# Attention, weight decoding and a first feed-forward pass: an order of issue computed in the kernel, in place of fixed offsets

## The chip, the cores and the metric

The kernel runs on one core of one Trainium2 chip. The metric is the time of one execution on the device in microseconds (us), the median of three runs. The engines are PE (TensorE; PEld are its weight loads), DVE (VectorE), ACT (ScalarE), POOL (GpSimd) and SP (SyncE, which here issues the DMAs).

## The reference

The result of a linear attention goes through a feed-forward layer with squared ReLU, and that through a mixture of eight experts whose gates come from a Sinkhorn iteration. All inputs are float32; only the weights of the first layer come as float64, which the kernel sees as pairs of 32-bit integers and turns into float32 itself ("decoding").

```python
# q, k, v: (4, 8, 576, 64), w_phi: (64, 128)
def phi(x):
    proj = x @ w_phi
    proj = proj - max(abs(proj), axis=-1)
    return concatenate([exp(proj), exp(-proj)], -1)
kv = einsum('bhsf,bhsd->bhfd', phi(k), v);  z = sum(phi(k), axis=2)
attn = einsum('bhsf,bhfd->bhsd', phi(q), kv) / (phi(q) @ z + 1e-6)
x = attn as (2304, 512)
x = relu(x @ w_in) ** 2 @ w_out              # w_in (512, 2048), w_out (2048, 512)
P = exp(x @ w_gate - max); 8 times: divide by row sums, by column sums, times N / E
out = sum over e of P[:, e] * (relu(x @ w1[e]) @ w2[e])   # 8 experts, 1024 hidden
```

## The kernel before

**Attention.** There are 16 units: four batches times four pairs of heads. A unit turns its keys (`turn_k`: PE transposes into pskT; high and low parts kh and kl), projects them (`proj_k`: PSUM tiles psk of two token tiles each; DVE takes the largest absolute value mk and subtracts it; ACT makes both exponentials in ek), sums them over the tokens (`kv_sum`: kvp with v, zp with ones) and turns the sums (`kv_turn`: kzp; kv, zs, z). Its queries are split (`split_q`: qst), turned (`turn_q`: psqT, qT), projected in four half-length pieces (`proj_q`: psq; POOL's all-reduce over partitions finds the maximum, DVE subtracts, ACT makes the exponentials eq). `numerators` makes, for each half of the tokens, psn and then psd; `recip` gathers the denominators from dn to comp by DMA, inverts them, writes them to DRAM (rden) and reads them back spread over the partitions (rb); `finish` multiplies (nm) and writes the high and low parts xh (ACT) and xl (DVE) of the next layer's input. Products in float32 precision are made of two or three products of high and low parts (`mm3`, lines 244 to 246).

**Decoding.** `decode` turns one 128-row block of a float64 weight into float32 with seven DVE instructions (lines 198 to 204); there are eight blocks for each of the four feed-forward passes. `split_w` makes high and low parts.

**The passes.** Each pass takes 512 of the 2048 hidden features. The first one works on eight halves of 288 tokens: `first_l1` makes four hidden tiles (48 matmuls), `first_l2` four output tiles (48), stored to `part` in DRAM. The passes behind it work on 512 tokens at a time, and the experts follow at line 874.

**The order.** An attention unit's ten steps are listed with offsets (`OFFS`), each unit `TU` = 17.54 us after the one before; the steps of all units are sorted by that time and emitted. Decoding follows the units named in `DECU`, right behind their `finish`. First-pass halves are emitted after them; `HOLD` ties some of them behind the key sums of a later unit. The framework then orders each engine's queue by its own estimate of times. PSUM for attention is two pools of three banks, shared in turn by all its tiles, and two banks for the first pass.

Of the kernel before, what the change touches and what calls it, by code (L numbers as in the profile page):

```python
# [10 lines left out]
I32 = mybir.dt.int32  # L11
# [9 lines left out]
def tile_features_attention__moe__sinkhorn_moe(  # L21
# [36 lines left out]
    GT = 2  # L58
    EQB = 4
    PAB, PCB = 3, 3  # L60
    NMB = 1
    EKB = 3
    STB = 1
    QTB = 1
    KTB = 1
    VAB = 2
    NQB = 1

    EARLY = {(0, 'kp'): -1, (0, 'qst'): -1}

    QSA = (0, 1)

    PIPE = (3, 4, 5,)
    TU = 17.54

    DECU = [1, 2, 3, 3, 4, 6, 7, 7, 9, 9, 9, 12, 12, 14, 14, 14]
    HOLD = {1: (4, "kvi"), 2: (12, "kvi"), 3: (15, "kvi"), 4: (12, "kvi"), 5: (10, "kvi")}
    OFFS = [(0, 'kT'), (3.4, 'kp'), (1.59, 'qst'), (3.0, 'qT'), (6.83, 'qp'), (9.28, 'kv'), (13.57, 'kz'), (23.24, 'num'), (31.33, 'rec'), (39.32, 'fin')]
# [12 lines left out]
    hp = hp1.enter_context(tc.tile_pool(name="hp1", bufs=1, side="right", reuse_waits="tile"))  # L91
    a1 = ctx.enter_context(ExitStack())
    ab = a1.enter_context(tc.tile_pool(name="ab", bufs=1, reuse_waits="tile"))
    pa = a1.enter_context(tc.tile_pool(name="pa", bufs=PAB, space=PSUM, reuse_waits="tile"))
    pc = a1.enter_context(tc.tile_pool(name="pc", bufs=PCB, space=PSUM, reuse_waits="tile"))
# [12 lines left out]
    nat = {}  # L108
# [7 lines left out]
    def load_q(u):  # L116
        if u >= NU:
            return
        t = ab.tile([P, NT2, D], F32, tag="nq", bufs=NQB, name="qnat")
        nc.sync.dma_start(t, heads(q, u).rearrange("h s d -> (h s) d").rearrange("(t p) d -> p t d", p=P))  # L120
        nat["q", u] = t

    def load_kv(u, src, nm, bufs):

        if u >= NU:
            return
        t = ab.tile([P, MT + 1, 2, D], F32, tag=f"n{nm}", bufs=bufs, name=f"{nm}nat")
        src = heads(src, u)
        for h in range(2):
            nc.sync.dma_start(t[:, :MT, h], src[h, : MT * P].rearrange("(p t) d -> p t d", t=MT))  # L130
        nc.sync.dma_start(t[:R0, MT], src[:, MT * P :].rearrange("h p d -> p h d"))
        nat[nm, u] = t

    def load_k(u):
        load_kv(u, k, "k", 2)

    def load_v(u):
        load_kv(u, v, "v", VAB)

    load_k(0)  # L140

    stg = ab.tile([P, 3, NF], F32, tag="ek", bufs=EKB, name="stg")
# [3 lines left out]
    load_q(0)  # L146
    load_v(0)
    load_k(1)
# [33 lines left out]
    def load_raw(p, w, i):  # L182
        t = wr.tile([P, FB, 2], I32, tag="raw", bufs=2, name=f"raw{p}_{w}_{i}")
        nc.sync.dma_start(t.rearrange("p f w -> p (f w)"), passes[p][w][i * P : (i + 1) * P, :])
        raws[p, w, i] = t

    def decode(p, w, i):


        raw = raws.pop((p, w, i))  # L190
        lo, hi = raw[:, :, 0], raw[:, :, 1]
        if i == 0:
            wf[p, w] = stage(p, w)
        sf = wf[p, w][:, i]
        s = sf.bitcast(I32)
        m = wr.tile([P, FB], I32, tag="dm", name="dm")
        mf = m.bitcast(F32)
        nc.vector.tensor_scalar(m, hi, 3, 0x3FFFFFF8, ALU.logical_shift_left, ALU.bitwise_and)
        nc.vector.scalar_tensor_tensor(m, hi, -0x40000000, m, ALU.bitwise_and, ALU.bitwise_or)
        nc.vector.tensor_scalar(s, m, -0x800000, None, ALU.bitwise_and)  # L200
        nc.vector.scalar_tensor_tensor(sf, lo.bitcast(U32), 2.0**-52, sf, ALU.mult, ALU.mult)
        nc.vector.tensor_add(sf, mf, sf)
        nc.vector.tensor_scalar(m, hi, 0x7FFFFFFF, None, ALU.bitwise_and)
        nc.vector.scalar_tensor_tensor(sf, m, float(897 << 20), sf, ALU.is_ge, ALU.mult)

    def fetch(p):

        if p >= NP:
            return
        if p >= N1:  # L210
            for w in range(2):
                wf[p, w] = stage(p, w)
                nc.sync.dma_start(wf[p, w], passes[p][w].rearrange("(k p) f -> p k f", p=P))
                yield
            return
        order = [(w, i) for w in range(2) for i in range(KD)]
        load_raw(p, *order[0])
# [8 lines left out]
    def split_w(p, w):  # L226
# [15 lines left out]

    def mm3(ps, ah, al, bh, bl, first, last):
        nc.tensor.matmul(ps, ah, bh, start=first, stop=False)  # L244
        nc.tensor.matmul(ps, ah, bl, start=False, stop=False)  # L245
        latest["pe"] = nc.tensor.matmul(ps, al, bh, start=False, stop=last).ins  # L246
# [13 lines left out]
    HB = {"hh": 5, "hl": 5, "r": 1}  # L260

    def split_square(pool, ps, n, nmax):

        r = pool.tile([P, nmax], F32, tag="r", bufs=HB["r"], name="r")
        nc.scalar.activation(r[:, :n], ps[:, :n], AF.Relu)  # L265
        nc.vector.tensor_mul(r[:, :n], r[:, :n], r[:, :n])
        gh = pool.tile([P, nmax], F32R, tag="hh", bufs=HB["hh"], name="gh")
        gl = pool.tile([P, nmax], F32R, tag="hl", bufs=HB["hl"], name="gl")
        latest["act"] = nc.scalar.copy(gh[:, :n], r[:, :n]).ins
        latest["dve"] = nc.vector.tensor_sub(gl[:, :n], r[:, :n], gh[:, :n].bitcast(F32)).ins  # L270
# [12 lines left out]
    def split_q(u):  # L283

        t = nat.pop(("q", u))
        st = ab.tile([P, NT2, 2, D], F32R, tag="st", bufs=STB, name="qst")
        (nc.scalar.copy if u in QSA else nc.gpsimd.tensor_copy)(st[:, :, 0], t)
        nc.vector.tensor_sub(st[:, :, 1], t, st[:, :, 0].bitcast(F32))
        load_q(u + NQB)
        return st  # L290

    def turn_q(st):
        tr = ab.tile([P, NT2, P], F32R, tag="qT", bufs=QTB, name="qT")
        for g in range(0, NT2, 4):
            n = min(4, NT2 - g)
            ps = pa.tile([P, 4, P], F32R, tag="pa", name="psqT")
            for i in range(n):
                nc.tensor.transpose(ps[:, i], st[:, g + i].rearrange("p a d -> p (a d)"), ident_r)
            nc.scalar.copy(tr[:, g : g + n], ps[:, :n].bitcast(F32))
        return tr  # L300

    def turn_k(u):
        t = nat.pop(("k", u))
        kh = ab.tile([P, S], F32R, tag="kT", bufs=KTB, name="kh")
        kl = ab.tile([P, S], F32R, tag="kl", bufs=KTB, name="kl")
        for i0, n in ((0, MT), (MT, 1)):
            ps = pa.tile([P, MT * P], F32, tag="pa", name="pskT")
            w = n * P if n > 1 else R0
            for i in range(n):
                r = P if n > 1 else R0  # L310
                nc.tensor.transpose(ps[:, i * P : i * P + r], t[:r, i0 + i].rearrange("p h d -> p (h d)"), ident[:r, :r])
            cs = slice(i0 * P, i0 * P + w)
            nc.scalar.copy(kh[:, cs], ps[:, :w])
            nc.vector.tensor_sub(kl[:, cs], ps[:, :w], kh[:, cs].bitcast(F32))
        load_k(u + 2)
        return kh, kl

    def proj_k(kT):

        eks = []  # L320
        for g in range(0, MT + 1, GT):
            n, r = (GT, P) if g < MT else (1, R0)
            ek = ab.tile([P, GT, 2, 2, NF], F32, tag="ek", bufs=EKB, name="ek")
            pk, nk = ek[:r, :n, :, 0], ek[:r, :n, :, 1]
            ps = pa.tile([P, GT, 2, NF], F32, tag="pa", name="psk")
            for i in range(n):
                cs = slice((g + i) * P, (g + i) * P + r)
                mm3(ps[:r, i], kT[0][:, cs], kT[1][:, cs], wdh, wdl, True, True)
            mk = ab.tile([P, GT, 2, 1], F32, tag="mk", bufs=2, name="mk")
            nc.vector.tensor_reduce(mk[:r, :n], ps[:r, :n], AX.X, ALU.max, apply_absolute_value=True)  # L330
            nc.vector.tensor_sub(pk, ps[:r, :n], mk[:r, :n].to_broadcast([r, n, 2, NF]))
            nc.scalar.activation(nk, pk, AF.Exp, scale=-1.0)
            nc.scalar.activation(pk, pk, AF.Exp)
            eks.append(ek)
        return eks

    def kv_sum(u, eks):


        t = nat.pop(("v", u))  # L340
        kvp = pc.tile([P, 512], F32, tag="pc", name="kvp")
        zp = pc.tile([P, 512], F32, tag="pc", name="zp")

        def rows(i, h):
            r = P if i < MT else R0
            return r, eks[i // GT][:r, i % GT, h].rearrange("p a f -> p (a f)")

        for g in range(0, MT + 1, 2):
            tiles = range(g, min(g + 2, MT + 1))
            for i in tiles:  # L350
                for h in range(2):
                    r, e = rows(i, h)
# [780 lines left out]
```

## Time and profile before

| | |
|---|---|
| runs | 2089.14, 2089.8, 2092.29 us; median 2089.8 |
| span of the profiled execution | 2090.2 us |
| its own time | not listed apart from the runs |
| PE busy, weight loads busy | 99%, 92% of the span |
| DVE, ACT, POOL busy | 83%, 42%, 37% |
| instructions | 31752 |

The span runs from the first to the last instruction of the profiled execution. Matmuls are pipelined and their ends are modelled, so PE's busy time contains waiting; the weight loads show better how densely it works. A row of a timeline gives start, length, engine, line, operation and the tiles (out<-in); a duration there reaches to the modelled end.

### The profile page before, as it was taken

What the parts mean: (1) busy time and instruction counts of PE and PEld (TensorE: products, weight loads), DVE (VectorE), ACT (ScalarE), POOL (GpSimd) and SP (SyncE); (2) the same over time, 40 slices, a digit from 0 to 9 for tenths busy, and PEclk for the clock granted to TensorE, in tenths of its full rate; (3) what the DMA queues carried; (4) which work ended last, traced back from release to release, by engine and by line L of the source; (5) the groups of instructions that cost most, each with busy time, mean ns of one, the idle gap of its engine ahead of it and who ended that gap; (6) DMA issues with size and microseconds to landing.
All of it is one profiled execution on the core that took longest, in us unless ns stands there. A gap on an engine that the chain in (4) does not pass through costs nothing.

```text
span 2090.2 us, 31752 instructions
## 1 busy us (share of the span) xinstructions
PE 2060.6 (99%) x12411; PEld 1924.6 (92%) x12411; DVE 1736.2 (83%) x2138; ACT 872.6 (42%) x1503; POOL 771.7 (37%) x428
## 2 busy tenths in 40 slices
PE   8999999999999999999999999999999999999998
PEld 5556679888999999999999999999999999999998
DVE  4888665766557898999989999899998989989986
ACT  6786754222233654343333434334333433433332
POOL 3343300010104544354534545345453444534431
PEclk9999999999999999999999999999999999999999
DMA  4444222110135566676666676676766776767663
GB/s 113 112 106 119 75 81 88 57 31 31 56 138 206 207 238 201 227 238 229 217 230 241 223 223 223 226 244 219 227 226 220 242 215 231 226 224 245 205 203 122
DMA packets 182949, 375.23 MB, mean 180 GB/s; under 512 B 73360, under 2 KB 113168, under 8 KB 182800
## 3 DMA queue, kind: packets, MB, share of 16 engines
q1 hardware_dynamic: 182800, 373.20, 54.4%
q8 instruction: 99, 1.62, 0.3%
q14 instruction: 50, 0.41, 0.1%
HBM read 348.67 MB, written 24.34 MB: 178 GB/s over the span
## 4 chain that ended last, share of the span: by engine, by line
PE 87%; DVE 7%; DMA 3%; ACT 1%; issue 1%; SPq 0%; POOL 0%; DVEq 0%; ACTq 0%
PE psa L874 31%; PE psb L874 31%; PE ps L244 6%; PE ps L245 6%; PE ps L246 6%; PE kvp L353 1%; DMA rb<-rden 1%; PE psn L409 1%; DVE acc L990 1%; DVE xl L610 1%; PE zp L360 1%; DMA rden<-comp 1%; DVE w2v L610 1%; PE psd L418 1%; PE psg L651 1%
## 5 line engine op out<-in xcount | busy, mean ns | idle before, releaser
L874 PE MATMUL psa<-xl,xh 128*128 128x384 f32 x2400 | 446.0, 335 | 3.5 <-DVE xl L610 2.5
L874 PE MATMUL psb<-xl,xh 128*128 128x384 f32 x2400 | 445.9, 335 | 3.5 <-DVE mu L949 1.8
L874 PEld LDWEIGHTS psb<-xl,xh 128*128 128x128 f32 x2400 | 419.1, 188 | 4.5 <-DVE mu L949 2.1
L874 PEld LDWEIGHTS psa<-xl,xh 128*128 128x128 f32 x2400 | 418.6, 188 | 4.7 <-DVE xl L610 2.9
L902 POOL TENSOR_TENSOR t<-r,r 128x768 f32<-128x768 f32 x96 | 207.2, 2158 | 500.5 <-DVE r L942 453.8
L902 POOL TENSOR_TENSOR t<-r,t 128x768 f32<-128x768 f32 x96 | 236.1, 2460 | 7.4 <-ACT r L946 1.9
L610 DVE TENSOR_TENSOR xl<-t,xl 128x768 fp32r<-128x768 f32 x128 | 186.9, 1460 | 1.8 <-ACT xl L609 1.6
L990 DVE TENSOR_TENSOR acc<-psb,acc 128x768 f32<-128x768 f32 x163 | 155.0, 951 | 35.6 <-PE psb L874 32.1
L990 DVE TENSOR_TENSOR acc<-psa,acc 128x768 f32<-128x768 f32 x161 | 153.1, 951 | 37.1 <-PE psa L874 33.9
L874 PE MATMUL psb<-xl,w2v 128*128 128x384 f32 x960 | 180.2, 334 | 0.0
L874 PE MATMUL psa<-xl,w2v 128*128 128x384 f32 x960 | 180.1, 334 | 0.0
L609 ACT CAST xl<-t 128x768 fp32r<-128x768 f32 x128 | 107.2, 838 | 156.6 <-POOL t L902 66.5
L874 PEld LDWEIGHTS psa<-xl,w2v 128*128 128x128 f32 x960 | 167.5, 188 | 0.0
L874 PEld LDWEIGHTS psb<-xl,w2v 128*128 128x128 f32 x960 | 167.5, 188 | 0.0
L609 ACT CAST xl<-r 128x768 fp32r<-128x768 f32 x96 | 80.4, 838 | 155.7 <-PE psa L874 77.4
L393 POOL PARTITION_ALL_REDUCE eq<-eq x64 | 90.7, 1460 | 138.4 <-ACT eq L392 138.4
L610 DVE TENSOR_TENSOR xl<-r,xl 128x768 fp32r<-128x768 f32 x96 | 135.9, 1416 | 1.4 <-ACT xl L609 1.4
L244 PE MATMUL ps<-xh,w0h 128*128 128x288 f32 (+3 forms) x384 | 130.5, 341 | 0.9 <-ACT r L265 0.8
L245 PE MATMUL ps<-xl,w0h 128*128 128x288 f32 (+3 forms) x384 | 129.0, 336 | 0.0
L246 PE MATMUL ps<-xh,w0l 128*128 128x288 f32 (+3 forms) x384 | 128.3, 337 | 0.0
L245 PE MATMUL ps<-gl,w1h 128*128 128x288 f32 (+3 forms) x384 | 126.9, 338 | 0.0
L246 PE MATMUL ps<-gh,w1l 128*128 128x288 f32 (+3 forms) x384 | 126.5, 338 | 0.0
(196 smaller groups left out, 3736.7 us busy)
## 6 DMA issues: line engine op xcount, KB each, us to landing
xl<-xv SPq DMA_DIRECT2D x329, 768.0 KB
wf<-in_moe_w_dram SPq DMA_DIRECT2D x32, 1024.0 KB
gate<-prT SPq DMA_DIRECT2D x45, 384.0 KB
xv<-xvs SPq DMA_DIRECT2D x14, 768.0 KB
raw<-in_moe_w_in_dram SPq DMA_DIRECT2D x16, 512.0 KB
raw<-in_moe_w_out_dram SPq DMA_DIRECT2D x16, 512.0 KB
xv<-xl SPq DMA_DIRECT2D x7, 768.0 KB
qnat<-in_q_dram SPq DMA_DIRECT2D x16, 288.0 KB
```

The source lines that it names most:

```text
L244: nc.tensor.matmul(ps, ah, bh, start=first, stop=False)
L245: nc.tensor.matmul(ps, ah, bl, start=False, stop=False)
L246: latest["pe"] = nc.tensor.matmul(ps, al, bh, start=False, stop=last).ins
L353: nc.tensor.matmul(kvp[h * D : (h + 1) * D, : 2 * NF], t[:r, i, h], e, start=(i == 0), stop=(i == MT))
L360: ins = nc.tensor.matmul(zp[q0 : q0 + 32, : 2 * NF], ones[:r, :32], e, start=(i < 2), stop=(i >= MT - 1))
L393: nc.gpsimd.partition_all_reduce(eq[:, 1], eq[:, 0], P, bass_isa.ReduceOp.absmax)
L409: nc.tensor.matmul(ps[h * D : (h + 1) * D, :HALF], kv[:, a, h * D : (h + 1) * D], eqs[2 * c + h][:, a], start=(a == 0), stop=(a == 1),)
L609: nc.scalar.copy(v[:, 0], src)
L610: nc.vector.tensor_sub(v[:, 1], src, v[:, 0].bitcast(F32))
L874: ins = nc.tensor.matmul(ps[:, x, :NB], w[:, wi, k, cs], b[:, bi, k], start=first and k + i == 0, stop=k == KH - 1 and i == 2, skip_group_ ...
L902: nc.gpsimd.tensor_tensor(t[nm], x, y, ALU.subtract)
L990: latest["dve"] = nc.vector.tensor_add(o, ps, o).ins
```

## The change

The steps of attention, the decoding of the first two passes' weights, and the first pass's work on six of the eight halves (five of them whole, of the sixth the hidden tiles) become steps of a list. Each has an engine, an assumed duration, what it needs, which PSUM slot it takes and a key. A scheduler in the kernel's Python simulates the engines: at each turn it takes the engine that can start first and gives it the ready step with the smallest key. The steps are emitted in that order, and each instruction of PE, DVE, ACT, POOL and SP is tied behind the one before it on its engine.

PSUM for attention becomes named tiles: two of two banks ("w") and two of one bank ("s"), each chosen by the scheduler; two banks ("m") stay for the first pass and the turned key sums.

The steps themselves change too:
- Keys: the rest of 64 tokens of both heads is loaded as one 128-row tile (with each head twice, side by side), so that five whole transposes do, and its projection takes two matmuls with `wks`. The load takes six DMAs where there were three; v's rest goes to zero-padded tiles, four DMAs where there were three. Maximum, subtraction and exponentials run on five and on four column blocks of 128 rather than on three pieces.
- Queries: projection, copy, all-reduce, subtraction and exponentials run once per head on 576 columns rather than on four pieces of 288. POOL makes the high part of q for all units.
- Numerators and denominators run once over both halves; denominators add up in PSUM, so one DMA gathers them. The copy of kv moves from DVE to ACT, those of z and of xh to POOL.
- Decoding gets another sequence of seven instructions; for the first pass it runs on two blocks at once. For the third and fourth passes' weights (decoded during the second and third), two of the seven steps go to POOL.
- One all-reduce on POOL runs at the start.

The core of the diff (removed functions are printed above):

```diff
+    class InOrder:
+        def __getattr__(self, name):
+            made = getattr(self.engine, name)
+            def op(*args, **how):
+                with ExitStack() as es:
+                    if ordered[0] and self.key in queued:
+                        es.enter_context(tc.issue_after(queued[self.key]))
+                    ins = made(*args, **how)
+                queued[self.key] = ins.ins
+                return ins
+            return op
+    V = InOrder(nc.vector, "dve")
+    A = InOrder(nc.scalar, "act")
+    G = InOrder(nc.gpsimd, "pool")
...
+    def decode_ops(lo, hi, sf, m, E):
+        s, mf = sf.bitcast(I32), m.bitcast(F32)
+        return [
+            lambda: V.tensor_scalar(m, hi, 0x7FFFFFFF, None, ALU.bitwise_and),
+            lambda: E.tensor_scalar(mf, mf, 2.0**-15, None, ALU.max),
+            lambda: V.tensor_scalar(m, m, 3, 0x3FFFFFF8, ALU.logical_shift_left, ALU.bitwise_and),
+            lambda: V.scalar_tensor_tensor(m, hi, -0x40000000, m, ALU.bitwise_and, ALU.bitwise_or),
+            lambda: V.tensor_scalar(s, m, -0x800000, None, ALU.bitwise_and),
+            lambda: V.scalar_tensor_tensor(sf, lo.bitcast(U32), 2.0**-52, sf, ALU.mult, ALU.mult),
+            lambda: E.tensor_add(sf, mf, sf),
+        ]
...
+    LAT = {"PE": 0.30, "DVE": 0.07, "ACT": 0.07, "POOL": 0.10, "SP": 0.07}
+    RINGS = {"w": 2, "s": 2, "m": 2}
+    EARLY, LATE = 15.02, 15.53
...
+    START = {"PE": 9.0, "DVE": 7.5, "ACT": 7.5, "POOL": 6.0, "SP": 3.5}
...
+        while len(made) < len(steps):
+            best = None
+            for e, todo in known.items():
+                at = [(room(s), s) for s in todo]
+                at = [(r, s) for r, s in at if r is not None]
+                if not at:
+                    continue
+                t = max(free[e], min(r for r, _ in at))
+                now = min(((s.key, s.index, max(r, t), s) for r, s in at if r <= t))
...
+                if best is None or now[2] < best[0]:
+                    best = now[2:]
+            t, s = best
...
+            free[e] = t + s.dur
+            s.end = t + s.dur + LAT[e]
+            if s.kb:
+                dma = max(dma, t + 1.7) + s.kb / 190.0
+                s.end = dma + 0.4
...
+        base = EARLY * min(u, 5) + LATE * max(0, u - 5)
+        def step(nm, *args, **how):
+            add(n(nm), *args, key=base + PHASE[nm], **how)
...
+        step("ldk", "SP", 0.36, loads_k, [n("tk", u - 1)], kb=295)
+        step("ldq", "SP", 0.06, loads_q, [n("qhi", u - 1), n("qlo", u - 1)], kb=295)
+        step("ldv", "SP", 0.24, loads_v, [n("A", u - 1)], kb=295)
...
+        step("A", "PE", 3.25, sums, [n("epA"), n("epB"), n("ldv")], [], ("s",), ([n("kvs")],), cols=1)
...
+        step("psn", "PE", 2.04, numerators, [n("qp0_"), n("qp1_"), n("kvc")], [], ("w",), ([n("nm")],), cols=1
+        )
+        step("psd", "PE", 1.2, denominators, [n("qp0_"), n("qp1_"), n("zw")], [n("psn")], ("s",), ([n("dn")],), cols=1)
+        step("cmp", "SP", 0.06, to_comp, [n("dn"), n("rd", u - 1)], kb=20)
+        step("rec", "DVE", 0.38, recip, [n("cmp")])
+        step("rd", "SP", 0.06, to_dram, [n("rec")], kb=20)
+        step("rb", "SP", 0.12, to_rows, [n("rd"), n("mul", u - 1)], kb=150)
+        step("mul", "DVE", 0.76, mul, [n("rb"), n("nm")])
+        step("xhi", "POOL", 0.75, xhi, [n("mul")] + raws_of)
+        step("xlo", "DVE", 0.75, xlo, [n("xhi")] + raws_of)
...
+                f"L1_{m}", "PE", 1.6, l1, xs_ + ["sl0", "sl2"], l2_of + ([f"L1_{m - 1}"] if m else []),
+                ("m",), ([f"re{m}"],), key=1e4 + 10 * seq,
...
+    plan = schedule()
+    for s in plan:
+        now[0] = s
+        s.emit()
+    ordered[0] = False
```

## Rows read from the trace of the kernel before

**Rows 1.** The page's slices (40 equal parts of the span), busy tenths of weight loads.

```profile
PEld 5556679888999999999999999999999999999998
```

**Rows 2.** Stretches: start:end, length, busy us and instructions of each engine, clock, DMA.

```profile
20.00:80.00 60.00, 58.17 (x465) 33.97 (x466) 40.78 (x92) 48.77 (x129) 28.83 (x23) 1.00 0.40 90
80.00:290.00 210.00, 202.30 (x1594) 132.10 (x1590) 167.09 (x345) 148.31 (x383) 71.87 (x57) 0.98 0.37 97
...
366.00:440.00 74.00, 74.00 (x373) 63.25 (x372) 46.78 (x83) 16.36 (x30) 0.00 (x0) 1.00 0.12 39
```

**Rows 3.** Timeline of PE, 0 to 60 us: start, length, what.

```profile
4.79 1.38 PE L311 MATMUL pskT<-ident,knat 128*128 128x128 f32 x5 [4.79 <-DMA knat<-in_k_dram]
...
20.53 0.80 PE L311 MATMUL pskT<-ident,knat 128*128 128x128 f32 x5
...
46.15 0.60 PE L311 MATMUL pskT<-ident,knat 128*128 128x128 f32 x4
46.68 2.53 PE L353 MATMUL kvp<-ek,vnat 128*64 128x256 f32 x20
49.14 0.27 PE L311 MATMUL pskT<-ident,knat 64*128 64x64 f32 x1
...
49.81 1.62 PE L360 MATMUL zp<-ek,ones 128*32 128x256 f32 x20
51.36 0.54 PE L298 MATMUL psqT<-ident_r,qst 128*128 128x128 f32 x4
...
52.33 0.28 PE L246 MATMUL psk<-wdh,kl 128*128 128x256 f32 x1
52.45 0.28 PE L244 MATMUL psk<-wdh,kh 128*128 128x256 f32 x1
...
54.15 1.19 PE L409 MATMUL psn<-eq,kv 128*64 128x288 f32 x8
55.27 0.40 PE L389 MATMUL psq<-qT,wks 128*128 128x288 f32 x1
55.51 0.29 PE L390 MATMUL psq<-qT,wks 128*128 128x288 f32 x1
...
59.14 0.69 PE L418 MATMUL psd<-eq,z 128*32 128x288 f32 x8
59.76 0.40 PE L389 MATMUL psq<-qT,wks 128*128 128x288 f32 x1
```

**Rows 4.** Timeline of PE: first and last of 48 first-pass matmuls back to back.

```profile
299.93 0.30 PE L244 MATMUL ps<-xh,w0h 128*128 128x288 f32 x1
...
306.14 0.29 PE L246 MATMUL ps<-xh,w0l 128*128 128x288 f32 x1
```

**Rows 5.** A stretch, instructions with tile ps (the first pass) alone: PE, PEld, DVE, ACT.

```profile
0.00:290.00 290.00, 57.41 (x336) 47.28 (x336) 0.00 (x0) 11.08 (x27) 0.99 0.39 100
```

**Rows 6.** DVE groups to 345 us: busy, mean ns, idle before; last: min/median/max.

```profile
L394 DVE TENSOR_TENSOR eq<-eq 128x288 f32<-128x288 f32 x64 | 33.7, 529 | 7.2 <-POOL eq L393 7.2
...
L439 DVE TENSOR_TENSOR nm<-nm,rb 128x576 f32<-128x576 f32 x16 | 12.6, 786 | 17.1 <-DMA rb<-rden 17.1
...
L442 DVE TENSOR_TENSOR xl<-nm,xh x16: 736/758/1282, 48.1 to 322.1; 128x576 fp32r<-128x576 f32 x16
```

**Rows 7.** Timeline of SP's issues at the start.

```profile
0.72 1.34 SPq L130 DMA_DIRECT2D knat<-in_k_dram  x2
2.10 0.63 SPq L131 DMA_DIRECT2D knat<-in_k_dram  x1
```

**Rows 8.** The page's costliest groups: POOL's two-input sums in the expert stage.

```profile
L902 POOL TENSOR_TENSOR t<-r,t 128x768 f32<-128x768 f32 x96 | 236.1, 2460 | 7.4 <-ACT r L946 1.9
```

**Rows 9.** The chain that ended last, 60 to 78 us: the transfers of one unit's denominators.

```profile
62.20 2.15 DMA comp<-dn
...
66.67 2.12 DMA rden<-comp
...
69.36 4.48 DMA rb<-rden
```

More of the change, by code (lines that the diff above doesn't have):

```diff
@@ L114, in heads @@
         return src[b, 2 * p2 : 2 * p2 + 2]
[L116 to L142, printed above, removed]
+    vrest = []
+    for j in range(2):
+        t = ab.tile([P, 2, D], F32, name=f"vrest{j}")
+        nc.gpsimd.memset(t, 0.0)
+        vrest.append(t)
+    onesh = ab.tile([P, 2, 32], F32, name="onesh")
+    nc.gpsimd.memset(onesh, 0.0)
+    for h in range(2):
+        nc.gpsimd.memset(onesh[h * R0 : (h + 1) * R0, h], 1.0)
+    stg = ab.tile([P, 3, NF], F32, tag="eka", bufs=1, name="stg")
     wphi = stg[:, 2]
@@ L280, in split_relu @@
         return gh, gl
[L283 to L335, printed above, removed]
@@ L514, in tile_features_attention__moe__sinkhorn_moe @@
-    bg = bg[1]
-    halves = [(t0, HALF) for t0 in range(0, NT, HALF)]
-    ahead = []
-    for i, (t0, n) in enumerate(halves[:-3]):
-        with ExitStack() as es:
-            if i in HOLD:
-                es.enter_context(tc.issue_after(U[HOLD[i][0]][HOLD[i][1]]))
-            g = ahead + first_l1(hp, t0, n, range(len(ahead), NFT))
-            ahead = first_l1(hp, *halves[i + 1], range(1)) if i in PIPE else []
-            first_l2(g, t0, n)
-    g5 = ahead + first_l1(hp, *halves[-3], range(len(ahead), NFT - 1))
@@ L526, in tile_features_attention__moe__sinkhorn_moe @@
-    with tc.issue_after(latest["act"]), tc.issue_after(latest["dve"]):
-        steps[-1][2]()
-    g5 += first_l1(hp, *halves[-3], range(NFT - 1, NFT))
+                A.copy(dst[:, c, t0 : t0 + n], ps[:, :n])
+    halves = [(t0, HALF) for t0 in range(0, NT, HALF)]
+    g5 = []
+    S_ = InOrder(nc.sync, "sp")
+    LAT = {"PE": 0.30, "DVE": 0.07, "ACT": 0.07, "POOL": 0.10, "SP": 0.07}
+    RINGS = {"w": 2, "s": 2, "m": 2}
+    EARLY, LATE = 15.02, 15.53
+    PHASE = {
+        "ldk": 11.0, "ldq": -22.8, "ldv": -15.0, "qhi": -8.3, "qlo": -4.7, "tq": -20.1, "qc0": -4.3, "qc1": 13.6,
+        "tk": -11.8, "kh": -2.0, "kl": -9.8, "kr": 0.4, "pkA": -6.5, "pkB": -9.4, "mkA": -8.8, "subA": 0.1,
+        "mkB": 0.8, "subB": -2.5, "enA": -0.7, "epA": 2.6, "enB": -3.9, "epB": 0.2, "A": 6.1, "kvs": 19.5,
[3 rows of a table added]
+        "rb": -1.9, "mul": 45.1, "xhi": 32.8, "xlo": 11.4,
+    }
@@ new lines, in tile_features_attention__moe__sinkhorn_moe, with __init__ @@
+    START = {"PE": 9.0, "DVE": 7.5, "ACT": 7.5, "POOL": 6.0, "SP": 3.5}
+    SOON = -29.83
+    SLACK = {"PE": 0.4, "DVE": 0.1, "ACT": 0.1, "POOL": 0.1, "SP": 0.0}
+    FREELY = "ws"
+    class Step:
+        def __init__(self, name, eng, dur, emit, needs, after, takes, frees, key, kb, cols):
+            self.name, self.eng, self.dur, self.emit = name, eng, dur, emit
+            self.needs, self.after, self.takes, self.frees = needs, after, takes, frees
+            self.key, self.kb, self.cols = key, kb, cols
+            self.start = self.end = None
```

658 lines of the change are left out of this document (469 added, 189 removed), and 3 rows, old and new, of the table PHASE.

## Prediction

> **What bounds the kernel now.** I read the page's slices first. From slice 6 onward TensorE's (PE's) weight loads are busy 8 or 9 tenths of every slice, in the first six 5 to 7 [rows 1]; the page says that a busy PE is not PE at its peak, so this row is the clue that there is time to win only in the first 350 us. The stretches say the same [rows 2]. From 366 to 440 us, in the second pass, PE is busy 74.00 of 74 us, VectorE (DVE) 46.78: PE sets the time. The only thing that the change does there and in the third pass is to give two steps of each weight decoding to GpSimd (POOL).
>
> So the question is the stretch up to 353.5 us, where the first feed-forward pass ends. In it 16 attention units (one batch, one pair of heads each) and the first pass's matmuls share PE.
>
> What PE needs I take from its timeline, from the start of one run to the start of the next, since printed lengths contain the pipeline's tail [rows 3]. A unit's key sums take 49.14 - 46.68 = 2.46 us (kvp) and 51.36 - 49.81 = 1.55 (zp). Half its numerators psn take 55.27 - 54.15 = 1.12, half its denominators psd 59.76 - 59.14 = 0.62. It needs the first two once, the last two twice: 2.46 + 1.55 + 2.24 + 1.24 = 7.49 us. Its other 41 instructions (15 psk, 9 psqT, 5 pskT, 4 kzp, 8 psq) I price at 0.12 each, the step from 52.33 to 52.45 in psk: 4.92. So a unit that never waited would cost 12.41 us.
>
> What it does cost: the first pass's 288-column matmuls, back to back, go from 299.93 to 306.14, 48 of them, so 6.21 / 47 = 0.132 us each [rows 4]. Before 290 us there are 336 [rows 5]: 44.4 us. PE starts at 4.79 [rows 3]. A unit had (290 - 4.8 - 44.4) / 16 = 15.05 us. **2.64 us of each unit, 42 us in all, go in small gaps between PE's pieces.** They aren't spread evenly: unit 1's key transposes start at 20.53 and unit 3's at 46.15, 12.8 us a unit, only 0.4 above the need [rows 3]. From 20 to 80 us DVE is busy 40.78 of 60 us, 68%; from 80 to 290, with more decoding and the first pass mixed in, 167.09 of 210, 80% [rows 2]. Most of the loss lies in that second stretch.
>
> **The change part by part.**
>
> *PE's work.* The key projection goes from 15 instructions to 12 + 2; the other kinds keep their number. 40 light ones at 0.12 make 4.80 us, 0.12 x 16 = 1.9 us less. Numerators and denominators run once per unit rather than as two halves in turn, so two changes of PE's column tiling go per unit. Behind psn, the first psq takes 55.51 - 55.27 = 0.24 us to the next instruction [rows 3], where 288 columns take 0.132 [rows 4]: 0.11 x 2 x 16 = 3.5 us less (bounds: nothing, as a wait would hide it, and 3.5, which I take, since PE is the scarce engine).
>
> *DVE's and ScalarE's work.* The query subtraction goes from four of 529 ns to two of 576 columns, like the 786 of nm [rows 6]: 0.54 us a unit. The key maxima and subtractions lose their tail pieces, the copies kv and z leave DVE, one three-operand step of each decoding becomes a two-operand one. All of that is off the path by itself; I book nothing for it, but it makes waits shorter.
>
> *The order.* All queues, also SyncE's DMA queue (SP), are now issued in an order computed from assumed durations: attention steps whole, first-pass groups where no attention step is ready. The work between 4.8 and 290 us stays, so the order can give back at most the lost 2.64 us a unit, and at least nothing. The nearest row of a well packed stretch is the 12.8 us pace, 0.4 lost; but there DVE is 68% busy and has little of the first pass. With DVE's load somewhat below the 80% of the long stretch, I expect a loss between the two and take 1.2 us: (2.64 - 1.2) x 16 = 23.0 us less.
>
> *The start.* SP takes 2.10 - 0.72 = 1.38 us for two issues, 0.69 each [rows 7]. Unit 0's keys were first. Now two loads of w_phi, one of q, four of v and six of k come ahead of the first key transpose: 13 x 0.69 = 9.0 us from 0.72, plus what now lies between the third issue's end (2.10 + 0.63 = 2.73) and the transpose at 4.79, 2.06: 11.8 us, 7.0 later. Meanwhile PE has the 17 query instructions, 2 us, and more of unit 1's: I take 4 us more (bounds 0, if the query half fills it, and 7.0).
>
> *The SP queue.* A unit issues 15 DMAs rather than 12: 10.4 us at 0.69, below the pace, so nothing, as long as the loads are issued early; where they aren't, the denominators' transfers queue behind them (rival 2).
>
> *POOL.* It gets the copy to xh and the widening of z, about 1 us a unit, on a queue that is busy 71.87 of 210 us [rows 2]: nothing, hidden by its own idle time; xl on DVE now waits for POOL instead of ScalarE. It also gets two steps of 16 decodings in the second and third passes. Its two-input step takes 2460 ns for 768 columns [rows 8], so two of 512 at most 3.3 us; a pass decodes eight blocks. That is hidden by a PE that has a whole block of tokens to do before it needs them: nothing. Were this cover gone, PE would wait for at most 16 x 3.3 = 52 us.
>
> The sum: -1.9 - 3.5 - 23.0 + 4 = -24.4 us. The profiled execution's span, 2090.2, lies inside the runs' times (2089.14 to 2092.29, median 2089.8), and no other time of it is listed, so I take the span as its time: **2066 us.**
>
> Bounds: with nothing lost any more, 2090.2 - 42.2 - 5.4 + 4 = 2047; with 0.4 lost, 2053; with all of 2.64 lost, 2089.
>
> **The rivals.**
> 1. *The order gives back little* (0.20). The assumed durations are not the chip's, and queues in which nothing may overtake wait for each other as now. For it: several engines at 70 to 80% are hard to interleave. Against: the 12.8 us stretch shows that this kernel's units can be packed. With 2.5 us lost: -1.9 - 3.5 - 2.2 + 4, so 2087.
> 2. *DVE stands at the denominators: slower than before* (0.14). For one unit comp takes 2.15 us to land, rden 2.12, rb 4.48; the chain runs from 62.20 to 73.84, 11.6 us [rows 9]. The plan counts 1.7 + 20/190 + 0.4 = 2.2 for each of the first two and 1.7 + 150/190 + 0.4 = 2.9 for the last, with the reciprocal 7.7. So mul can stand at the head of DVE's queue some 4 us too early, and behind it are the subtractions that PE's projections and numerators of the next units need. In the kernel now DVE waits 17.1 us for rb in all [rows 6]. It decides from the point where this wait exceeds DVE's idle fifth, 2.6 us a unit: then 1.4 of the 4 us reach PE. With the old 2.64 kept: need 12.41 - 0.12 - 0.22 = 12.07, pace 12.07 + 2.64 + 1.4 = 16.1 against 15.05, 17 + 4 us more: 2111.
> 3. *DVE and POOL hold each other up* (0.05). xl takes 758 ns as a rule and 1282 at worst [rows 6], so something stretches it now and then, and 1 us a unit of copying is moved to POOL. If DVE stood for all of it and PE with it, 16 us of the 24.4 were gone: 2082. The Trainium skill (SBUF — State Buffer, "SBUF: two separate sides") says that a DVE instruction with two inputs in SBUF and a POOL instruction that reads SBUF share a port pair under an exclusive lock, and the one that comes second blocks entirely; by that rule each overlap holds the later instruction for the rest of the first, and the sum would be 2082; by the median of the row it stays 2066.
> 4. *Nearly all of the loss returns* (0.08): 2047 to 2050.
>
> The forecast itself, with 0.4 to 2.0 us lost (2051 to 2079), has 0.53.
>
> **How the numbers follow.** 0.2%, about what a measurement of this kernel can tell from no change, is 4.2 us: 2085.6 to 2094. Faster: the forecast, rivals 3 and 4, and half of rival 1: 0.53 + 0.05 + 0.08 + 0.10 = 0.76. Same: the other half of rival 1, 0.10. Slower: rival 2, 0.14. The range, 2048 to 2092, leaves out rival 2 and the tip of rival 4; its ends are the bounds of the lost time, and at the upper end 7 us for the start.
>
> **What would show it.** If I am right, PE's first 512-column matmul comes about 25 us earlier than it does now; neighbouring units' key transposes lie 12.5 to 14 us apart early on; the first key transpose is near 11 us; weight loads reach 7 tenths in slices 2 to 6; the passes behind keep their length. DVE waiting for rb for more than 40 us in all shows rival 2; xl and the subtractions at a median over 1 us, rival 3; the old gaps, rival 1. I am wrong if decoding comes so late that it holds the first pass, or if its groups are used up before the last units end: then PE stands for their chain, up to 11.6 us.

## The result, and the profile after

The changed kernel takes 2070.88 us (four runs, 2070.43 to 2071.35) beside 2091.05 for the kernel before on the same chip: a ratio of 0.9904 (95% interval 0.989 to 0.9918), 20.2 us less. The forecast was 2066, its range 2048 to 2092. The profiled execution took 2070.59 us with a span of 2068.5; all of what follows is read from it.

First the page's slices of the changed kernel (weight loads), then stretches (columns as in [rows 2]), then of the late one the first pass's matmuls alone (PE's busy time and instructions, clock, DMA).

```profile
PEld 4577798888999999999999999999999999999998
```

```profile
20.00:80.00 60.00, 49.71 (x431) 31.77 (x435) 53.87 (x74) 41.53 (x70) 25.29 (x18) 0.93 0.53 133
12.70:110.60 97.90, 81.35 (x677) 55.09 (x676) 82.53 (x115) 63.47 (x106) 41.77 (x29) 0.93 0.48 120
110.60:213.90 103.30, 103.26 (x952) 77.97 (x953) 90.78 (x166) 75.71 (x144) 43.35 (x36) 1.00 0.50 127
366.00:440.00 74.00, 74.00 (x373) 63.21 (x372) 47.84 (x82) 16.25 (x30) 23.05 (x20) 1.00 0.12 37
```

```profile
110.60:213.90 103.30, 24.86 (x168) 1.00 0.50 127
```

Beside [rows 1], weight loads are busier in the third to sixth slice and less busy in the first and seventh. From 366 us on PE is as full as in [rows 2], with POOL at 23.05 us where it had none. The first pass's last 288-column matmul starts at 333.36 us and not at 353.55, the experts' first at 642.30 and not at 662.43. So the whole gain lies in the first 350 us, as the prediction said, and the passes behind it neither gain nor lose.

What no sum of the prediction had is the contrast of the second and third stretch. They hold units 0 to 6 and units 7 to 13, from key transposes to key transposes. In the first PE is busy 81.35 of 97.9 us, DVE 82.53; in the second PE is busy 103.26 of 103.3.

The timeline of PE (start, length) shows the beginning, unit 1, and one unit of the late stretch, from its key transposes at 140.18 to the next ones at 154.92:

```profile
11.52 1.26 PE L241 MATMUL psw<-ident_r,qst 128*128 128x128 f32 x8 [11.52 <-DVE qst L106]
...
12.71 1.29 PE L241 MATMUL psw<-ident,knat 128*128 128x128 f32 x5
...
18.85 0.85 PE L241 MATMUL psw<-ident,knat 128*128 128x128 f32 x5 [0.73 <-ACT eq L106]
21.33 0.88 PE L241 MATMUL psw<-ident_r,qst 128*128 128x128 f32 x8 [1.63 <-DVE qst L106]
...
140.18 0.71 PE L241 MATMUL psw<-ident,knat 128*128 128x128 f32 x5
...
142.41 2.16 PE L241 MATMUL psw<-eq,kv 128*64 128x288 f32 x16
144.50 1.18 PE L241 MATMUL pss<-eq,z 128*32 128x288 f32 x16
145.60 1.08 PE L241 MATMUL pss<-eka,vnat 128*64 128x256 f32 x8
...
149.33 0.80 PE L241 MATMUL psw<-qT,wks 128*128 128x288 f32 x4
...
154.92 0.71 PE L241 MATMUL psw<-ident,knat 128*128 128x128 f32 x5
```

From start to start, as in the prediction: numerators 144.50 - 142.41 = 2.09 us, denominators 1.10, key sums 149.33 - 145.60 = 3.73, and 40 light pieces at 0.12 are 4.80. A unit needs 11.72 us. The late unit took 14.74 with 24 first-pass matmuls in it (168 in the seven units), 3.17 us, so 11.57: nothing is lost there.

With these prices (and 0.132 us for a 288-column matmul, 0.227 for a 512-column one; for before those of [rows 3, 4]) each matmul of a stretch can be priced, and what is left of the stretch is PE's loss, gaps and slowed matmuls together. Stretches run from PE's first matmul to unit 7's key transposes, from there to unit 14's, and on to the first pass's last matmul. These ends, first in the kernel before, then in the changed one:

```profile
108.59 0.80 PE L311 MATMUL pskT<-ident,knat 128*128 128x128 f32 x5
...
238.96 0.86 PE L311 MATMUL pskT<-ident,knat 128*128 128x128 f32 x5
...
353.55 0.30 PE L246 MATMUL ps<-gh,w1l 128*128 128x288 f32 x1
```

```profile
110.64 0.77 PE L241 MATMUL psw<-ident,knat 128*128 128x128 f32 x5 [0.52 <-ACT eq L106]
...
213.94 0.71 PE L241 MATMUL psw<-ident,knat 128*128 128x128 f32 x5
...
333.36 0.30 PE L241 MATMUL ps<-gh,w1l 128*128 128x288 f32 x1
```

| us | PE's first matmul | priced work | lost, units 0 to 6 | lost, units 7 to 13 | lost, rest | last matmul |
|---|---|---|---|---|---|---|
| before | 4.8 | 303.6 | 20.6 | 17.9 | 6.7 | 353.5 |
| after | 11.5 | 291.9 | 26.6 | -1.0 | 4.4 | 333.4 |

6.7 us later at the start, 11.7 less work, 15.2 less loss: -20.2 us. The new order removes the loss of the late units (18.9 us) and makes that of the early ones 6 us larger.

### The profile page after: what moved, and what is told of

Same layout as the page of the kernel before. It is cut to its first block, busy times and chain, and to the rows that moved or that the text cites. A ratio compares the mean times of both kernels' runs of the same rounds, so it can differ in the third digit from the quotient of the medians.

```text
span 2068.5 us, 31436 instructions
## 1 busy us (share of the span) xinstructions
PE 2026.5 (98%) x12395; PEld 1926.4 (93%) x12395; DVE 1706.3 (82%) x1978; ACT 840.1 (41%) x1289; POOL 822.5 (40%) x469
## 4 chain that ended last, share of the span: by engine, by line
PE 91%; DVE 5%; DMA 2%; ACT 1%; issue 1%; SPq 1%; POOL 0%; DVEq 0%; POOLq 0%; ACTq 0%
PE psa L1246 32%; PE psb L1246 32%; PE ps L241 19%; PE pss L241 3%; PE psw L241 3%; SPq L106 1%; PE psg L1023 1%; DVE acc L1362 1%; DMA rb<-rden 1%; DVE xl L982 1%; DVE acc L1392 0%; DVE xh L982 0%; DVE hv L982 0%; DMA xl<-xv 0%; ACT eq L106 0%
## 5 line engine op out<-in xcount | busy, mean ns | idle before, releaser
L1055 POOL TENSOR_TENSOR s<-wf 128x512 f32<-128x512 f32 x32 | 44.3, 1385 | 216.2 <-DVE xvs L982 82.4
```

Of the source, the lines that this page charges most:

```text
L1055: nc.gpsimd.tensor_tensor(s1, a(2, 1), a(2, 2), ALU.add)
```

## The experiments

Each is an edit of the changed kernel. The table repeats the accounting for the profiled execution of each; the "early" and "late" losses are those of the two columns above. The accounting itself scatters by some 2 us between executions: a run whose edit acts only behind the first pass (E9) has its last matmul 2.4 us later than the changed kernel.

| | median us | ratio to before (95%) | PE's first | early loss | late loss | last matmul |
|---|---|---|---|---|---|---|
| changed kernel | 2070.88 | 0.9904 (0.989 to 0.9918) | 11.5 | 26.6 | -1.0 | 333.4 |
| E1 order free | 2110.96 | 1.0096 (1.0073 to 1.012) | 12.1 | 33.3 | 25.2 | 372.6 |
| E2 SP's durations | 2073.09 | 0.9915 (0.9893 to 0.9936) | 11.5 | 26.4 | 2.9 | 333.8 |
| E3 keys first | 2070.73 | 0.9903 (0.9878 to 0.9928) | 5.7 | 25.2 | 6.3 | 330.7 |
| E4 xh on ACT | 2070.67 | 0.9898 (0.987 to 0.9926) | 11.5 | 23.9 | -1.0 | 331.7 |
| E5 DVE +10.5 early | 2076.36 | 0.9925 (0.991 to 0.994) | 12.2 | 30.0 | -0.3 | 339.3 |
| E6 DVE +12 late | 2075.14 | 0.9922 (0.9907 to 0.9937) | 11.8 | 26.2 | 1.5 | 336.6 |
| E7 PE +8.1 early | 2074.05 | 0.9916 (0.9899 to 0.9932) | 11.6 | 21.6 | -1.2 | 334.2 |
| E8 PE +9.3 late | 2077.48 | 0.9936 (0.9921 to 0.9951) | 12.0 | 25.0 | -1.5 | 338.6 |
| E9 decoding on DVE | 2072.21 | 0.9906 (0.9891 to 0.9921) | 11.5 | 27.3 | -0.9 | 335.8 |
| E10 earlier start | 2067.18 | 0.988 (0.9864 to 0.9897) | 6.8 | 28.6 | -1.1 | 332.6 |
| E11 measured durations | 2058.62 | 0.9846 (0.9832 to 0.9861) | 6.8 | 21.5 | 1.8 | 323.2 |
| E12 later due times | 2067.78 | 0.989 (0.9874 to 0.9906) | 6.9 | 29.1 | 1.6 | 331.0 |

**E1, order free.** The same steps, emitted in the plan's order, but no instruction is tied behind the one before it; the framework orders the queues again.

```
-    ordered = [True]
+    ordered = [False]
```

> The steps, their number and the sequence in which they are emitted stay as in the changed kernel; only the ties that keep each engine's queue in that sequence are dropped, so that the framework orders the queues by its own estimate again. Theory: the order is what returned the gaps (14 us of the 20), so the time goes back by 8 to 16 us, to 2079 to 2087, and key transposes of neighbouring units lie over 15.5 us apart. Rival: the merged steps alone did it, and the ties are of no weight: within 3 us of 2071.

2110.96 us, slower than the kernel before, though PE's work per unit is the smaller one, and far above the 2079 to 2087 expected. Key transposes lie 21 us apart from unit 7 to unit 10 and 17 behind; those of units 12 to 14:

```profile
215.18 0.77 PE L241 MATMUL psw<-ident,knat 128*128 128x128 f32 x5
232.19 0.77 PE L241 MATMUL psw<-ident,knat 128*128 128x128 f32 x5
249.00 0.71 PE L241 MATMUL psw<-ident,knat 128*128 128x128 f32 x5
```

On these steps the ties are worth 40 us, 26 of them in the late stretch: the smaller steps by themselves win nothing in a free order. The PSUM tiles are still those that the plan chose for its own order, so the 40 us hold that mismatch too; the new steps in a free order with tiles of its own were not tried.

**E2, SP's durations.** The plan counts 0.06 to 0.36 us for SP's steps; here it gets what the trace shows, and transfers that start 1.6 us behind the end of their issue.

```
-                dma = max(dma, t + 1.7) + s.kb / 190.0
+                dma = max(dma, t + s.dur + 1.6) + s.kb / 190.0
-        step("ldk", "SP", 0.36, loads_k, [n("tk", u - 1)], kb=295)
+        step("ldk", "SP", 3.84, loads_k, [n("tk", u - 1)], kb=295)
...
-        step("rb", "SP", 0.12, to_rows, [n("rd"), n("mul", u - 1)], kb=150)
+        step("rb", "SP", 1.10, to_rows, [n("rd"), n("mul", u - 1)], kb=150)
```

> The scheduler is told what an issue on the DMA queue takes on the chip (0.4 to 0.64 us each rather than 0.06); nothing else is changed. In the changed kernel the key transposes of unit 7 come 17 us later than its plan has them, and those of unit 14 19 us. Theory A (the DMA queue's issue times make the plan slip, rival 2 of the prediction in a small form): a plan that knows them slips less, 4 to 10 us less time, 2061 to 2067. Theory B (the slip comes from a nearly full VectorE in the first 105 us): no more than 3 us either way, 2068 to 2074.

No gain: with SP's true durations in the plan the early stretch loses as much (26.4 us). That these durations were too short in the plan is not what costs the time there.

**E3, keys first.** Unit 0's keys are loaded ahead of w_phi, q and v.

```
+        if u == 0:
+            steps["ldk0"].key = -30.0
```

> Unit 0's keys are loaded ahead of its queries and v, as in the kernel before. The prediction's term for the start was 4 us (bounds 0 and 7). If the start is on the path, PE's key chain begins 3 to 4 us earlier and 2 to 4 us come off, 2067 to 2069. Rival: VectorE paces the first 105 us anyway, so an earlier start is swallowed by its queue: within 1.5 us of 2071.

The first key transposes move from 12.71 to 5.7 us, and the median stays. What unit 0 wins, the plan that follows from the new key loses again (late loss 6.3). The four runs scatter from 2066.11 to 2073.68 us, and the table's losses are those of the fastest of them.

**E4, xh on ACT.** POOL loses its copy in the feed of the passes.

```
-            G.tensor_copy(xh[:, p2, ts_], x["nm"])
+            A.copy(xh[:, p2, ts_], x["nm"])
-        step("xhi", "POOL", 0.75, xhi, [n("mul")] + raws_of)
+        step("xhi", "ACT", 0.68, xhi, [n("mul")] + raws_of)
```

> The high half of x is copied by ScalarE again rather than by POOL (and planned there). Rival 3 of the prediction: VectorE is held up by POOL's copies; while xh was copied, VectorE's instructions took 3.6 us more in all than at their shortest. If that is on the path, 2 to 4 us come off (2067 to 2069). If not, ScalarE's extra 11 us are hidden too: within 2 us of 2071. If ScalarE's queue is the tighter one, it is 3 us or more slower.

The xl subtractions on DVE, min/median/max ns, first in the changed kernel, then here:

```profile
L106 DVE TENSOR_TENSOR xl<-nm,xh x16: 744/748/1843, 52.3 to 274.1; 128x576 fp32r<-128x576 f32 x16
```

```profile
L106 DVE TENSOR_TENSOR xl<-nm,xh x16: 744/754/760, 52.9 to 272.5; 128x576 fp32r<-128x576 f32 x16
```

On xl the stretched ones are gone, and the time is the same. But the copy was not what stretched them. The 1843 ns of the changed kernel fall beside POOL's all-reduce (POOL's timeline, then DVE's):

```profile
66.50 1.60 POOL L106 CAST xh<-nm 128x576 fp32r<-128x576 f32 x1 [1.94 <-DVE nm L106]
68.08 2.13 POOL L106 PARTITION_ALL_REDUCE eq<-eq  x1
```

```profile
68.13 1.84 DVE L106 TENSOR_TENSOR xl<-nm,xh 128x576 fp32r<-128x576 f32 x1 [0.56 <-POOL xh L106]
```

The all-reduces stay in E4, and single instructions of qst, eq and nm still take up to 1390, 1391 and 1850 ns. Over xl and these three, what exceeds the median is 9.4 us in the changed kernel and 5.9 here: rival 3's effect exists, and 3.5 us less of it change nothing at the end. A kernel without any of it was not tried.

**E5 to E8, shadow prices.** E5 and E6 make DVE's key maxima twice in units 0 to 6 (10.5 us more) or from unit 8 on (12 us); E7 and E8 make PE's denominator matmuls twice in the same units (8.1 and 9.3 us); the second making starts the sums anew, so the result stays. The E6 and E8 edits differ only in `u >= 8`.

```
-                V.tensor_reduce(mk[:, :m], x["psp"][g], AX.X, ALU.max, apply_absolute_value=True)
+                for _ in range(2 if u < 7 else 1):
+                    V.tensor_reduce(mk[:, :m], x["psp"][g], AX.X, ALU.max, apply_absolute_value=True)
...
-            for a in range(2):
+            for a in (0, 1, 0, 1) if u < 7 else (0, 1):
```

> In units 0 to 6 each of the two key maxima is taken twice, 0.82 + 0.69 us more of VectorE per unit, 10.5 us in all; the plan, the order and the result stay. Theory: VectorE, near full there, sets the first 105 us, so 7 to 10.5 us are added to the changed kernel's 2070.9. Rival: it is latency and in-order waiting without a bound engine, so that gaps swallow it: under 4 us.

> The same in units 8 to 15: 12 us more of VectorE, at 110 to 260 us. Theory: PE sets this stretch and VectorE has slack there, so at most 4 us are added. Rival: the two engines are locked in one order and VectorE's extra work goes to the end: 8 to 12 us.

> In units 0 to 6 the denominators' matmuls run twice, 1.16 us more of PE per unit, 8.1 us in all; plan, order and result stay. Theory: PE waits for VectorE there, so at most 3 us are added; if the extra work also keeps the granted clock up, which fell to half in three stretches of 13.7 us together before 100 us in the changed kernel, it may cost nothing or less. Rival (PE bound from the start): 6 to 8 us.

> The same in units 8 to 15: 9.3 us more of PE at 110 to 260 us. Theory: PE is the bound there, with first-pass work filling its gaps, so 7 to 9.3 us are added. Rival: PE has gaps that swallow it, under 3 us.

Read by the last matmul, E5 costs 6.0 of 10.5 us, E6 3.3 of 12, E7 0.8 of 8.1, E8 5.2 of 9.3 (by the medians 5.5, 4.3, 3.2, 6.6). E5 and E8 fall between the two outcomes expected, 7 us or more and a gap that swallows it; E6 and E7 are near the 4 and 3 us that their theories allowed. So early PE has room: in E7 the early loss falls by 5 us, the added matmuls lie in the gaps. A little over half of what is added to DVE there comes out at the end. Late it is the other way round; E8's late units go to 15.7 us from 14.75:

```profile
200.98 0.71 PE L241 MATMUL psw<-ident,knat 128*128 128x128 f32 x5
216.70 0.71 PE L241 MATMUL psw<-ident,knat 128*128 128x128 f32 x5
```

The early stretch hangs more on DVE and on the chains tied to it, the late one more on PE. E5 can't tell DVE's load from the chain, since its added maxima lengthen both.

**E9, decoding on DVE.** The two decoding steps of the third and fourth passes go back from POOL.

```
-        for op in decode_ops(raw[:, :, 0], raw[:, :, 1], wf[p, w][:, i], m, G):
+        for op in decode_ops(raw[:, :, 0], raw[:, :, 1], wf[p, w][:, i], m, V):
```

> The decoding for the third and fourth feed-forward pass goes back from POOL to DVE; nothing else is changed. Theory (the prediction's step that books nothing for it): either engine has room under the matmuls of the second half, so the time stays within 1.5 us of 2070.9. Rival: the decoding on POOL is part of the gain, or has cost some of it: the time moves by 3 us or more, and the stretch after the first pass is longer or shorter by as much.

1.3 us more, inside the bound set; the profiled execution has its 2.4 us already at the end of the first pass, before the edit acts. PE is full from 366 us on in either. The prediction's zero for this step stands.

**E10, earlier start.** The order stays as planned; POOL's all-reduce goes behind the memset, unit 0's q is cast on ACT, and its keys are loaded ahead of v.

```
-    G.partition_all_reduce(warm[:, 1:], warm[:, :1], P, bass_isa.ReduceOp.absmax)
...
-    nc.gpsimd.memset(wd, 0.0)
+    zeroed = nc.gpsimd.memset(wd, 0.0).ins
+    with tc.issue_after(zeroed):
+        G.partition_all_reduce(warm[:, 1:], warm[:, :1], P, bass_isa.ReduceOp.absmax)
...
-            G.tensor_copy(st[:, :, 0], x["nq"])
+            (A.copy if u == 0 else G.tensor_copy)(st[:, :, 0], x["nq"])
...
-        step("ldk", "SP", 0.36, loads_k, [n("tk", u - 1)], kb=295)
+        step("ldk", "SP", 0.36, loads_k if u else loads_v, [n("tk", u - 1)], kb=295)
```

> The planned order stays the same, but POOL's warming all-reduce is issued behind the memset of the decoding tile, unit 0's query cast is done on ACT at the same place of the order, and unit 0's keys are loaded ahead of its values. TensorE should begin near 7 us and not at 11.5. Theory A (the late start lies on the path that sets the end): 3 to 6 us less, 2065 to 2068 us, and the first pass's last matmul earlier by as much. Theory B (the early stretch, tied to DVE's order, swallows it, as with the keys first): within 1.5 us of 2070.9, and unit 7's key transpose stays near 110 us.

The reason for this run is the timeline of POOL in the changed kernel, and below it that of DVE:

```profile
1.53 0.29 POOL masks.py:199 TENSOR_SCALAR_AFFINE_SELECT ident<-ident 128x128 f32<-128x128 f32 x1 [0.29 <-POOL vrest L129]
8.09 0.41 POOL L106 PARTITION_ALL_REDUCE warm<-warm  x1 [6.27 <-issue]
...
8.47 0.38 POOL L141 MEMSET stg<- 128x256 f32 x1
...
9.11 0.66 POOL L106 CAST qst<-qnat 128x576 fp32r<-128x576 f32 x1
```

```profile
8.88 0.97 DVE L143 COPY stg<-stg 64x128 f32<-64x128 f32 x2 [6.79 <-DMA knat<-in_k_dram]
...
10.72 0.75 DVE L106 TENSOR_TENSOR qst<-qnat,qst 128x576 fp32r<-128x576 f32 x1
```

POOL stands 6.27 us with nothing to wait for, ahead of an all-reduce whose value nobody uses. Behind it in the queue are the memset of a tile that DVE's copy needs and the high part of q, then DVE's subtraction, then PE at 11.52. (The DVE row names a DMA as its releaser; it starts as the memset ends, at 8.85.) In E10 the memset goes first and PE starts at 6.82:

```profile
1.86 0.31 POOL L140 MEMSET stg<- 128x256 f32 x1
8.20 0.41 POOL L106 PARTITION_ALL_REDUCE warm<-warm  x1 [6.02 <-issue]
```

The median falls by 3.7 us, but the intervals overlap, and in the profiled executions 4.7 us at the first matmul become 2.6 at unit 7's key transposes (108.02) and 0.7 at the last matmul. That the late start cost something is likely; how much of the 6.7 us is not settled.

**E11, measured durations.** E10's start (the keys moved by a key of -18), and a plan remade with the durations from the trace: key sums 3.72 for 3.25, wide decoding steps 0.97 for 0.68, POOL's cast 0.95 for 0.75, SP as in E2, and so on. The times at which the plan lets each engine begin change with the start (PE 6.0 for 9.0, POOL 9.0 for 6.0), and the decoding's due times are 20 us later.

```
-    START = {"PE": 9.0, "DVE": 7.5, "ACT": 7.5, "POOL": 6.0, "SP": 3.5}
+    START = {"PE": 6.0, "DVE": 6.0, "ACT": 5.0, "POOL": 9.0, "SP": 2.0}
...
+            s.dur = TRUE.get(s.name.rstrip("0123456789"), s.dur)
+            if s.name.startswith("op"):
+                j, o = s.name[2:].split("_")
+                s.dur = (WIDE if int(j) < 8 else NARROW)[int(o)]
...
-        0: 40.7, 2: 70.4, 4: 70.6, 6: 94.6, 8: 128.2, 9: 141.2, 10: 154.2, 11: 167.1, 12: 180.1, 13: 193.1,
+        0: 60.7, 2: 90.4, 4: 90.6, 6: 114.6, 8: 148.2, 9: 161.2, 10: 174.2, 11: 187.1, 12: 200.1, 13: 213.1,
...
```

> The start of the run before, and a plan remade with the durations that the trace of the changed kernel shows for POOL, ACT, DVE, PE and SP (key sums 3.72 for 3.25, wide decoding steps 0.97 for 0.68 and so on), with the decoding's due times 20 us later. Theory A (the plan slips 17 us by unit 7 because its durations are too short, and its order ties engines to work that is not ready there): unit 7's key transpose comes 5 to 12 us earlier, 2059 to 2066 us. Theory B (the early stretch is full of DVE's work whatever the plan takes its steps for): 2069 us or more, unit 7's key transpose within 3 us of 110.

2058.62 us, a ratio of 0.9846 to before, clear of the changed kernel's interval and better than both kernels. Its stretches (units 0 to 6, units 7 to 13) and two rows of PE:

```profile
8.00:102.50 94.50, 81.20 (x698) 53.74 (x696) 77.34 (x109) 65.61 (x111) 39.37 (x31) 0.95 0.50 132
102.50:203.90 101.40, 99.93 (x909) 75.35 (x910) 92.64 (x159) 73.26 (x136) 45.89 (x36) 1.00 0.48 123
```

```profile
102.49 0.77 PE L242 MATMUL psw<-ident,knat 128*128 128x128 f32 x5 [0.73 <-ACT eq L106]
...
218.61 0.60 PE L242 MATMUL psw<-ident,knat 128*128 128x128 f32 x4
```

Unit 7 comes 5.5 us earlier than in E10, and the early loss is 7.1 us smaller. DVE is busy 77.34 of 94.5 us there, 82%, about as before the change of plan. Of decoding and the splitting of weights it has 28 instructions in that stretch, where the changed kernel and E10 have 33. E10's units 0 to 6:

```profile
8.00:108.00 100.00, 85.43 (x677) 57.22 (x677) 82.82 (x116) 63.72 (x106) 42.46 (x33) 0.88 0.49 127
```

PE stands idle 14.6 us there and 13.3 in E11, so most of the 7.1 us are not waits: PE's matmuls run slower in E10, at a granted clock of 0.88 beside 0.95. In executions of one and the same order a lower clock went with more of PE busy and no longer stretch (the last section), which speaks for the plan as the cause; no run changes the plan at the same clock.

**E12, later due times.** E10 with E11's due times alone.

> The run with the earlier start (2067.2 us) with one thing added: the decoding's due times are 20 us later, as in the run with measured durations (2058.6 us), while the plan keeps the durations that it had. Theory A (what the plan takes its steps for is what gave the 8.6 us between these two): 2065 to 2069 us, unit 7's key transpose near 108 us. Theory B (the later due times alone give it, because decoding then no longer goes ahead of attention's steps on DVE): 2057 to 2061 us, unit 7's key transpose near 102 us. In between, both have a part.

2067.78 us, as E10: the due times by themselves give nothing. E2 had shown the same of SP's durations. The ten runs of E10 and E12, 2065.85 to 2070.11 us, all lie below the changed kernel's four, which speaks for a small gain from the start. What is left for E11's 8.6 us over E10 is the remade plan as a whole: the durations of DVE, PE, ACT and POOL, the engines' assumed start times and the place of unit 0's key load, alone or together with SP's durations and the due times. They were not tried one by one.

## Why the prediction was right, and where not

**What bounds, and where: right.** All of it came in the first 350 us, and the passes behind stayed as full as they were. POOL's part of the decoding is hidden (E9).

**PE's work: mis-sized, too small.** The terms were -1.9 and -3.5, 5.4 us; priced from the rows it is 11.7. Key sums in one run take 3.73 where the two runs of [rows 3] take 2.46 + 1.55 = 4.01, which the sum did not book at all; numerators and denominators take 3.19, close to the 3.48 - 0.22 that it had. Per unit that is 0.12 for the light piece, 0.28 and 0.29: 11.0 of the 11.7.

**The order: right in kind, too large, and wrong in its distribution.** The term was 23.0 us; measured 15.2. The loss was not left evenly at 1.2 us a unit. It is gone in the late units, which the prediction had named as the place of most of the loss, and 26.6 us in the early ones, which it took for well packed by the pace from unit 1 to unit 3 in [rows 3]. By price the early units of the kernel before already lost 20.6 us; that pace was of two favourable units. The rule that a loss between 0.4 and the old one would remain had no mechanism behind it. What the runs show is that the early loss grows with DVE's work (E5) and shrinks with a plan remade from the trace (E11); that engines of a fixed order stand behind steps that the plan took for ready fits both, but is argued.

**The sum: near in part by luck.** The work's term was 6.3 us too small, the order's 7.8 too large and the start's 2.7 too small, and these errors partly cancel: 2066 lies only 5 us below the measured time. One figure of the forecast's band doesn't follow from its own sum: with 0.4 us lost it is 2053, not 2051.

**The start: about the size, with the wrong cause.** Booked +4 with bounds of 0 and 7; PE's first matmul comes 6.7 us later. The SP issues are about as long as booked (0.64 us each for 0.69), the last load of unit 0's keys ends its issue at 9.13 us. But PE waited for q, which stood behind POOL's warming all-reduce, a line of the diff that the prediction passed over. The Trainium skill (GPSIMD Engine Reference, "2.1 Instruction dispatch") says that the first call of a freshly loaded GpSimd kernel pays about 6 us of code loading that no instruction in the profile shows; the 6.27 and 6.02 us above agree. In the kernel before, POOL's first all-reduce starts at 17.12 us, behind a wait of 15.36 for ACT that could cover such a load; no run shows whether it does.

**Rival 2, DVE at the denominators: not seen.** The groups of DVE and the view of xl's tile above answer to [rows 6]:

```profile
L106 DVE TENSOR_TENSOR nm<-nm,rb 128x576 f32<-128x576 f32 x16 | 13.2, 822 | 11.0 <-DMA rb<-rden 11.0
L106 DVE TENSOR_TENSOR xl<-nm,xh 128x576 fp32r<-128x576 f32 x16 | 14.0, 876 | 3.6 <-POOL xh L106 3.6
```

DVE waits 11.0 us for rb in all, less than the 17.1 of before, and far from the 40 that would have decided.

**Rival 3, DVE and POOL: small.** The median of xl is 748 ns, the mean 876: 16 x 0.128 = 2 us of stretching. The same reckoning gives 3.1 us for eq, 3.2 for qst and 1.1 for nm, 9.4 in all, where the rival had 16. By the rule of the Trainium skill (SBUF — State Buffer, "SBUF: two separate sides") the later of two such instructions blocks entirely; the xl of 1843 ns began 0.05 us behind POOL's all-reduce and was held up, but ended at 69.97, before POOL's end at 70.21 (POOL's spans are rough). E4 takes 3.5 of the 9.4 us away and wins nothing.

**Rival 1, an order that gives little,** holds for the first 110 us alone, where the new order gives nothing. Its reason, that the assumed durations are not the chip's, fits E11.

**The signs.** The first 512-column matmul comes 19.5 us earlier (326.76 for 346.29), not 25. Key transposes lie 14.0 us apart on average early on, but unevenly, from 6 to 21 us; the first come at 12.71 rather than near 11; weight loads reach 7 tenths from the third slice on, which the prediction, counting from 0, calls slice 2, as it said.

## What to carry to other kernels

An order computed ahead and tied in place rests on its assumed durations: take them from a trace of the kernel that it orders, by shape and by engine, and remake it. Here a plan remade so, with its start and due times, won 8.6 us more. Judge packing by pricing every matmul of a stretch, not by the pace of a pair of units, since pieces of other units are shifted into and out of it. Look at what stands in a queue behind a first use of an engine's code, even where its result isn't needed.

## What the runs showed of the hardware

POOL's first all-reduce starts some 6 us after POOL's last work with no wait shown, whether a memset stands before it or behind it (6.27 and 6.02 us).

A DVE instruction with two inputs can take over twice its usual time beside POOL's all-reduce over partitions (1.84 us for 0.75, at 68.13 us above).

The granted clock of PE, between the levels of 1.2 and 2.4 GHz, fell in the early stretch, where PE has gaps: to a mean of 0.93 in the changed kernel (12.70 to 110.60 us), where the kernel before had 1.00 from 20 to 80 us [rows 2] and fell later, to 0.57 from 156 to 164 us, which is 3.4 us of full clock at most out of its late loss of 17.9. From 110.6 to 213.9 us, with PE full, it is 1.00 in the changed kernel.

The profile's clock counts as full where nothing is recorded, and at the start nothing is. The steps of the matmuls show what was granted there, first in E2:

```profile
21.27 0.41 PE L241 MATMUL pss<-wdl,kh 128*128 128x256 f32 x1
21.48 0.41 PE L241 MATMUL pss<-wdh,kl 128*128 128x256 f32 x1
...
33.19 0.28 PE L241 MATMUL pss<-wdl,kh 128*128 128x256 f32 x1
33.31 0.28 PE L241 MATMUL pss<-wdh,kl 128*128 128x256 f32 x1
```

From start to start a 128x256 matmul takes 0.21 us and later 0.12. So E2 runs at the lower level from 11.5 to 29.7 us, where its records begin, though the row of 11.5 to 110.6 us reads 0.97. In the changed kernel the step falls to 0.12 at 16.5 us. With these starts added, the lower level holds 18.6 us of the early stretch in the changed kernel, 25.0 in E2, 30.3 in E10 and 13.9 in E11.

What it costs can be read from E6, E8 and E9, which have the changed kernel's instructions and order up to unit 7. The lower level holds 26.8, 18.8 and 24.0 us of their early stretches and 18.6 of the changed kernel's; from PE's first matmul to unit 7's key transposes they take 98.8, 97.5, 99.9 and 99.1 us. So 8 us more at the lower level have no clear price there: PE is busy 84.49 of 99.1 us in E6 and 82.52 in the changed kernel, the slower matmuls lying where PE would wait. In E3 the time does rise as the clock falls: 2066.11, 2069.62, 2071.84 and 2073.68 us at means of 0.998, 0.997, 0.996 and 0.995.
